# Attention and two feed-forward layers on one core: tails read back in halves, output weights copied two products later, outputs placed between products

## The chip, the cores and the metric

One core of one Trainium2 chip runs one program. The metric is the device time of an execution in microseconds, median of three runs. Products of full precision are built from split operands: every 32-bit operand is kept as a rounded half ("hi") and a remainder ("lo"), and a product takes three matmuls, hi·hi, hi·lo and lo·hi.

## The reference

```python
attn_out = _attn_ref(q, k, v, M_prev, z_prev, beta)        # 4 x 8 heads, 576 tokens, 64 wide
x = attn_out.transpose(0, 2, 1, 3).reshape(2304, 512)
h = x @ w_in;  x = np.maximum(0.01 * h, h) @ w_out         # first layers, 512 -> 2048 -> 512
a = x @ w_a;   b = x @ w_b
out = (a * b) @ w_out2                                     # second layers, 512 -> 1536 -> 512
```

## The kernel before

The program has three stages: attention (to about 200 us), the first layers (`moe1`, to about 583 us) and the second layers (`moe2`, to the end). TensorE runs the products, ScalarE (ACT) copies and rounds, VectorE (DVE) and GpSimd (POOL) add and subtract, and SyncE (SP) issues nearly all transfers. The order on each engine is the order in which the Python program emits the instructions; nothing reorders them. A counter, `tick()`, advances by one for each product or output on TensorE, and `after(k, ...)` emits a step k ticks later.

The 2304 tokens are worked in two parts, part one with 1024 tokens and part two with 1280.

**First layers.** `SETS` lists nine sets, each a part and one or two groups of 256 hidden columns. A set runs its inward products (kind "u", 12 matmuls each, chunk by chunk of 512 tokens) and then its outward products (kind "o"). The activations `x` of part two have a tail, the tokens from 1024 on, which lives in columns 0 to 1023 of a tile "g3". The same tile is the fourth hidden tile of the two-group sets, so the tail is kept in DRAM (`xkept`, 1 MB) and read back for each later set of part two: in `fourth(n)`, called when that set begins (L1476). The tail's first reader is the fifth inward product of such a set, the third chunk. The last set of part two keeps its tail in a tile inside `xs1` (`sums.first`).

**Second layers.** For each part, `slots(pr)` lists the order of work on TensorE. For q = 0 to 11 (even q: w_b, odd q: w_a of group g = q // 2) the letters 1 to 7 are seven products of 256 by 512 by 512 in Strassen's scheme with Winograd's sums, 6 matmuls each; "O" is one output of 128 tokens of the group before (also 6 matmuls, with the output weights), "T" a product of part two's last 256 tokens. After part one's q = 11 come the 8 outputs of group 5, O(5,0) to O(5,7), and then part two begins with two T.

- A product's result is summed on DVE (L1364) or, for product 1, copied from PSUM on ACT (L1368). When a block of an odd q is complete, DVE multiplies it with the block of w_b (L1391), and `finish` makes its halves: ACT rounds one tick later (L1348), DVE subtracts two ticks later (L1349). Product 7 completes block (f=1, c=1), 2 completes (0,0), 3 completes (1,0), 4 completes (0,1). An output of the first 512 tokens needs (0,0) and (1,0).
- The halves of a group lie in two of the three tiles hl0, hl1 and qs0, taken in rotation by `shared()`, so the second tile of a group is one that the outputs of the group before still read.
- `weights.final(g, ...)` brings the output weights of group g: two reads of 256 KB from DRAM into one small stage (L357), each followed by a copy on ACT (L358) and a subtraction on GpSimd (L359). It is called when the outputs of group g-2 are done.
- `Matrices.make` builds the split matrices of the later q on ACT (L1266) and GpSimd (L1263, L1270), writes them to DRAM (2 MB each, L1273, L1275), and part two reads them back (`fetch`, 2 MB each, L1291, L1292).
- The sums and halves of part two's inputs are jobs ("1b", "6", "5", "7c234"), put on a list at products of q = 11 and taken one a slot; their halves use ACT (L1174, L1175) and GpSimd (L1180, L1184).
- `xs1` holds the tail of part two in columns 0 to 2047 (`sums.tail`, made at the first product of q = 4, L1144 and L1148), and three inputs of products in the columns behind. The tail's first reader is part two's first T.

Of the kernel before, what the change touches and what calls it, by code (L numbers as in the profile page):

```python
# [11 lines left out]
F32 = mybir.dt.float32  # L12
F32R = mybir.dt.float32r
# [99 lines left out]
def f32(ap):  # L113
    return ap.bitcast(F32)
# [3 lines left out]
def attention_moe_moe2(ctx: ExitStack, tc, kqT, qn, vn, m_prev, beta, w_in, w_out, w_a, w_b, w_o2, out):  # L118
# [28 lines left out]
    def after(k, fn):  # L147
        now[1] += 1
        heapq.heappush(tasks, (now[0] + k, now[1], fn))
# [7 lines left out]
    class Weights:  # L157
# [194 lines left out]
        def final(self, g, t, stage):  # L352
            w = t.rearrange("p (s f c) -> p s f c", s=2, f=2)
            for f in range(2):
                k = max(0, self.staged - now[0])
                self.staged = now[0] + k + 8
                after(k, lambda f=f: nc.sync.dma_start(f32(stage), self.saved[g][:, f]))  # L357
                after(k + 5, lambda f=f: nc.scalar.copy(w[:, 0, f], f32(stage)))  # L358
                after(k + 6, lambda f=f: nc.gpsimd.tensor_tensor(w[:, 1, f], f32(stage), f32(w)[:, 0, f], ALU.subtract))  # L359
            return w  # L360

    SETS = [(0, [0]), (1, [0, 1]), (0, [1, 2]), (1, [2, 3]), (0, [3, 4]), (1, [4, 5]), (0, [5, 6]), (0, [7]), (1, [6, 7])]
# [693 lines left out]
    def shared(tag=None):  # L1056
        if tag is None:
            tag = gtags[count["g"] % len(gtags)]
            count["g"] += 1
        t = main.tile([P, 2 * WIDE], F32R, tag=tag, bufs=1, name=tag) if isinstance(tag, str) else tag()  # L1060
        return t.rearrange("p (s c) -> p s c", s=2)
# [57 lines left out]
    class Sums:  # L1119
# [8 lines left out]
        def first(self):  # L1128
            t = self.t1 = main.tile([P, 8192], F32R, tag="xh0", bufs=1, name="xs1")
            self.place(t, self.FIRST)  # L1130
            self.tail = t[:, 0:2048].rearrange("p (s k c) -> p s k c", s=2, k=4)
            self.g4 = t[:, 2048 : 2048 + 2 * WIDE].rearrange("p (s c) -> p s c", s=2)

        def second(self):
# [164 lines left out]
    def slots(pr):  # L1299

        tiles = (PARTS[pr + 1] - PARTS[pr]) // 128
        out = []
        for q in range(12):
            g, a = divmod(q, 2)
            if pr:
                text = ("16572O3O4OOOOTT", "1O6O5OO7234TT")[a] if g else ("TT1657234", "1657234TT")[a]
            else:
                text = ("16572O3O4OO", "1O6O5OO7234")[a] if g else "1657234"
            o, f = a * (tiles - 4), 0
            for x in text:  # L1310
                if x == "O":
                    out.append(("O", g - 1, o))
                    o += 1
                elif x == "T":
                    out.append(("T", q, f))
                    f += 1
                else:
                    out.append(("P", q, x))
        return out + [("O", 5, i) for i in range(tiles)]

    def moe2(ps, sums, mats, spare):
# [7 lines left out]
        for pr in range(2):  # L1329
# [10 lines left out]
            def into(g, f):  # L1340
                t = cts.setdefault(g, [None, None])
                if t[f] is None:
                    t[f] = shared()
                return t[f]

            def finish(g, f, c, gf):
# [100 lines left out]
    with tc.manual_schedule():  # L1447
        jobs = []

        def run(n):  # L1450
            for _ in range(min(n, len(jobs))):
                jobs.pop(0)()

        xh[0] = part_tile(main, "xh", 0, (2, 4), F32R)
        ps = ctx.enter_context(tc.tile_pool(name="ps", bufs=1, space=PSUM))
        with tc.tile_pool(name="att", bufs=1) as att:
            gates = attention(att, Plan(ps))
        sb = ctx.enter_context(tc.tile_pool(name="moe", bufs=1))
        weights.pool, weights.own, weights.n, weights.top = sb, 4, 4, 4
        weights.done |= {("own", i, h) for i in range(2) for h in range(2)}  # L1460
        x0, x1 = xh[0], sb.tile([P, 8192], F32R, tag="xh1", bufs=1, name="xh").rearrange("p (s k c) -> p s k c", s=2, k=4)
        xkept = dram.tile([P, 2, 1024], F32, tag="xkept", name="xkept")
        sums = Sums()
        credit = [0.0]
        t3s, ys = [None], {}

        def fourth(n):
            if n == len(SETS) - 1:
                sums.first()
                t = sums.g4  # L1470
            else:
                t = shared(lambda: sb.tile([P, 2 * WIDE], F32R, tag="g3", bufs=1, name="g3"))
            if SETS[n][0]:
                t3s[0] = t
                if n > 1:
                    nc.sync.dma_start(f32(t)[:, :, 0:1024], xkept)  # L1476
            return t

        def convert(w, rate):
            credit[0] += w * 1.33e-3 * rate * 2  # L1480
            while credit[0] >= 1:
                credit[0] -= 1
                weights.step()

        def x_of(s, kt, c):
            return t3s[0][:, s, kt * 256 : kt * 256 + 256] if c.start >= 1024 else x1[:, s, kt, c]

        def piece(kt, c, eng):
            nc.scalar.copy(x_of(0, kt, c), xf[1][:, kt, c])
            after(1, lambda: eng.tensor_tensor(x_of(1, kt, c), xf[1][:, kt, c], f32(x_of(0, kt, c)), ALU.subtract))  # L1490

        def y(pr):
            if pr not in ys:
                ys[pr] = part_tile(main, "xf", pr)
            return ys[pr]

        t31 = fourth(1)
        jobs += [lambda kt=kt, c=c: piece(kt, c, (nc.vector, nc.gpsimd)[kt % 2]) for c in chunks(1) for kt in range(4)]
        weights.spare += [("plain", m, h) for m in range(12) for h in range(2)] + [("last", g, h) for g in range(6) for h in range(2)]
        m = 0  # L1500
        xs = [lambda s, kt, c: x0[:, s, kt, c], x_of]
        for n, kind, g, w in moe1(ps, gates, lambda n: t31 if n == 1 else fourth(n), xs, y):
            if n == 1 and m == 0:
                m = 1
                nc.sync.dma_start(xkept, f32(t31)[:, :, 0:1024])
            if n == len(SETS) - 1:
                if (kind, g) == ("u", 6) and m == 1:
                    m = 2
                    raw = sb.tile([P, 2 * WIDE], F32, tag="g3", bufs=1, name="raw")
                    mats = Matrices(raw[:, 0:2048])  # L1510
                    mats.load(0)
                    mats.when = now[0]
                if kind == "o":
                    m += 1
                if m == 9:
                    mats.make(1)
                if m == 3:
                    while weights.items or weights.quarter or weights.spare:
                        weights.step()
                        tick()  # L1520
                    spares = [main.tile([P, 512], F32, tag=f"gf{i}", bufs=1, name="gf") for i in range(3)]
                    t = main.tile([P, 2 * WC], F32, tag="wraw", bufs=1, name="gf")
                    spares += [t[:, 0:WC], t[:, WC : 2 * WC]]
                    spares += [main.tile([P, WC], F32, tag=k, bufs=1, name="gf") for k in ("wh", "wa", "wr")]
                    sums.second()
                    mats.make(0)
                    steps = sums.jobs(ys[0], {f"S{i + 1}": spares[i * 2 : i * 2 + 2] for i in range(4)}, nc.vector)
                    jobs += [steps[k] for k in "a1b65c2d7"]
            run(2 if n == 0 else 1)
            convert(w, 0.7 if n == 0 else 0.74)  # L1530
        spares.append(raw[:, 2048:2560])
        y1 = ys[1]
        run(len(jobs))
        jobs += [steps[k] for k in "34"]
        for pr, (kind, q, k) in moe2(ps, sums, mats, spares):
            if (pr, kind, q, k) == (0, "P", 4, "1"):
                sums.last(y1)
                r = mats.raw
                steps = sums.jobs(y1, {
                    "S1": [y1[:, k, 512:1024] for k in range(2)],  # L1540
                    "S2": [r[:, k * 512 : k * 512 + 512] for k in range(2)],
                    "S3": [y1[:, k * 2 : k * 2 + 2, 1024:1280] for k in range(2)],
                    "S4": [r[:, k * 512 : k * 512 + 512] for k in range(2, 4)],
                }, nc.gpsimd)
            if (pr, kind, q, k) == (0, "P", 6, "1"):
                jobs += [steps["d"], steps["a"]]
            if (pr, kind, q) == (0, "P", 11):
                jobs += [steps[x] for x in {"1": "1b", "6": "6", "5": "5", "4": "7c234"}.get(k, "")]
            run(1)
        while tasks:  # L1550
            tick()
# [74 lines left out]
```

## Time and profile before

| | us |
|---|---|
| median of 3 runs | 1008.35 (1007.85 to 1008.89) |
| profiled execution, whole | 1009.16 |
| its span, first to last instruction | 1007.4 |
| TensorE busy in the span | 990.8 (98%) |
| granted TensorE clock, mean | 0.997 |

Matmuls of 512 columns overlap in the pipeline: each lasts 0.39 us in the trace and the next one starts 0.227 us after it. A place where TensorE loses time is therefore read from the distance between two starts. In a row of the timeline, a bracket tells how long the engine was idle before the instruction and what ended that.

### The profile page before, as it was taken

What the parts mean: (1) busy time and instruction counts of PE and PEld (TensorE: products, weight loads), DVE (VectorE), ACT (ScalarE), POOL (GpSimd) and SP (SyncE); (2) the same over time, 40 slices, a digit from 0 to 9 for tenths busy, and PEclk for the clock granted to TensorE, in tenths of its full rate; (3) what the DMA queues carried; (4) which work ended last, traced back from release to release, by engine and by line L of the source; (5) the groups of instructions that cost most, each with busy time, mean ns of one, the idle gap of its engine ahead of it and who ended that gap; (6) DMA issues with size and microseconds to landing.
All of it is one profiled execution on the core that took longest, in us unless ns stands there. A gap on an engine that the chain in (4) does not pass through costs nothing.

```text
span 1007.4 us, 14598 instructions
## 1 busy us (share of the span) xinstructions
PE 990.8 (98%) x5266; PEld 799.0 (79%) x5266; DVE 771.1 (77%) x1500; ACT 425.1 (42%) x947; POOL 378.6 (38%) x386
## 2 busy tenths in 40 slices
PE   9999999999999999999999999999998999999998
PEld 4666666788888888888888887887886888888887
DVE  6999999799797989798998764786665717647646
ACT  7988887465434333433335344323323122201201
POOL 6778777341111111111112787767577001001000
PEclk9999999999999999999999999999998999999999
DMA  7344432233535343435245337436554422432412
GB/s 233 103 134 139 139 124 67 71 108 109 154 111 169 114 136 106 172 111 156 88 154 178 115 136 256 176 132 230 219 197 180 178 94 95 167 115 94 144 45 105
DMA packets 41432, 139.88 MB, mean 139 GB/s; under 512 B 4752, under 2 KB 5520, under 8 KB 36752
## 3 DMA queue, kind: packets, MB, share of 16 engines
q1 hardware_dynamic: 41216, 138.95, 40.6%
q8 instruction: 41, 0.67, 0.3%
q14 instruction: 31, 0.25, 0.1%
q10 hardware_dynamic: 144, 0.00, 0.0%
HBM read 98.57 MB, written 40.37 MB: 138 GB/s over the span
## 4 chain that ended last, share of the span: by engine, by line
PE 86%; DVE 5%; DMA 3%; POOL 2%; ACT 2%; issue 1%; SPq 0%; ACTq 0%; POOLq 0%; DVEq 0%
PE b L373 24%; PE b L375 24%; PE b L374 24%; PE b L724 4%; PE b L803 3%; PE b L665 3%; PE b L775 1%; DVE gf L1364 1%; DMA g<-xkept 1%; PE b L596 1%; DMA qraw<-in_qn 1%; PE b L693 1%; DMA bhi<-saved 1%; DVE gf L1391 1%; ACT p L619 1%
## 5 line engine op out<-in xcount | busy, mean ns | idle before, releaser
L1364 DVE TENSOR_TENSOR gf<-b,gf 128x512 f32<-128x512 f32 x148 | 101.1, 688 | 77.1 <-PE b L375 66.2
L1426 DVE TENSOR_TENSOR xf<-b,xf 128x512 f32<-128x512 f32 (+1 forms) x91 | 62.2, 684 | 71.5 <-PE b L375 71.5
L1044 POOL TENSOR_TENSOR hl<-gf,hl 128x512 fp32r<-128x512 f32 (+1 forms) x20 | 28.3, 1415 | 234.9 <-ACT hl L1043 229.6
L359 POOL TENSOR_TENSOR w<-bhi,w 128x512 fp32r<-128x512 f32 x24 | 34.8, 1449 | 177.0 <-ACT w L358 167.6
L373 PE MATMUL b<-xh,w 128*128 128x512 f32 x256 | 100.9, 394 | 0.0
L374 PE MATMUL b<-xh,w 128*128 128x512 f32 x256 | 99.7, 390 | 0.0
L375 PE MATMUL b<-xh,w 128*128 128x512 f32 x256 | 99.7, 389 | 0.0
L373 PE MATMUL b<-xs,bhi 128*128 128x512 f32 (+1 forms) x216 | 79.4, 367 | 2.1 <-ACT gf L1368 1.7
L1077 ACT ACTIVATE gf<-b 128x512 f32<-128x512 f32 (+1 forms) x76 | 42.0, 553 | 89.5 <-PE b L375 88.5
L374 PE MATMUL b<-xs,bhi 128*128 128x512 f32 (+1 forms) x216 | 79.1, 366 | 0.0
L374 PE MATMUL b<-xs,ahi 128*128 128x512 f32 (+1 forms) x216 | 79.0, 366 | 0.0
L373 PE MATMUL b<-xs,ahi 128*128 128x512 f32 (+1 forms) x216 | 79.0, 366 | 0.0
L375 PE MATMUL b<-xs,blo 128*128 128x512 f32 (+1 forms) x216 | 79.0, 366 | 0.0
L375 PE MATMUL b<-xs,alo 128*128 128x512 f32 (+1 forms) x216 | 78.9, 365 | 0.0
L619 ACT ACTIVATE p<-p,stat 128x512 f32<-128x512 f32 (+3 forms) x128 | 71.0, 559 | 5.5 <-DVE stat L673 5.2
L646 POOL TENSOR_SCALAR p<-p,stat,keep 128x128 f32<-128x128 f32 (+3 forms) x95 | 61.0, 655 | 17.4 <-DVE stat L634 12.8
L261 ACT ACTIVATE wh<-wraw 128x512 f32<-128x512 f32 x64 | 42.7, 667 | 55.3 <-DMA wraw<-in_w_o 21.7
L373 PE MATMUL b<-hl,w 128*128 128x512 f32 (+1 forms) x176 | 65.2, 370 | 0.0
L374 PE MATMUL b<-hl,w 128*128 128x512 f32 (+1 forms) x176 | 65.1, 370 | 0.0
L375 PE MATMUL b<-hl,w 128*128 128x512 f32 (+1 forms) x176 | 65.1, 370 | 0.0
L673 DVE CUSTOM_DVE_ANT_0 p<-b,mask 128x512 f32<-128x512 f32 (+3 forms) x128 | 57.6, 479 | 5.4 <-PE b L665 5.0
L375 PE MATMUL b<-w,hl 128*128 128x512 f32 (+1 forms) x145 | 57.0, 393 | 2.0 <-DVE hl L1349 2.0
(204 smaller groups left out, 2669.0 us busy)
## 6 DMA issues: line engine op xcount, KB each, us to landing
wraw<-in_w_in SPq DMA_DIRECT2D x16, 512.0 KB, 4.0
wraw<-in_w_out SPq DMA_DIRECT2D x16, 512.0 KB, 3.4
qraw<-in_qn SPq DMA_DIRECT2D x8, 768.0 KB, 6.9
wraw<-in_w_b SPq DMA_DIRECT2D x12, 512.0 KB, 3.5
wraw<-in_w_a SPq DMA_DIRECT2D x12, 512.0 KB, 3.7
plain<-wa SPq DMA_DIRECT2D x24, 256.0 KB, 3.7
wraw<-in_w_o SPq DMA_DIRECT2D x12, 512.0 KB, 3.6
raw<-plain SPq DMA_DIRECT2D x12, 512.0 KB, 3.5
```

The source lines that it names most:

```text
L261: nc.scalar.activation(t["h"], self.raw[n][:, :, 1].bitcast(F32), AF.Abs)
L359: after(k + 6, lambda f=f: nc.gpsimd.tensor_tensor(w[:, 1, f], f32(stage), f32(w)[:, 0, f], ALU.subtract))
L373: nc.tensor.matmul(outp, l_hi, r_hi, start=start, stop=False)
L374: nc.tensor.matmul(outp, l_hi, r_lo, start=False, stop=False)
L375: nc.tensor.matmul(outp, l_lo, r_hi, start=False, stop=stop)
L619: nc.scalar.activation(t, t, AF.Exp, bias=s[:, 0, col : col + 1], scale=-1.0, accum_out=s[:, 1, col : col + 1])
L646: ENG[eng].tensor_scalar(live[p], live[p], stats[w % 3][:, 3, col : col + 1], k, ALU.mult, ALU.mult)
L673: nc.vector.tensor_tensor_reduce(one(p, [P, wd]), plan.tiles[banks[j]][:, c : c + wd], mask[:, off : off + wd], -0.125, BIG, ALU.add, ALU. ...
L724: nc.tensor.transpose(tt[0:kw, n * 128 : n * 128 + 128], live[name][:, kt * 128 : kt * 128 + kw], ident)
L1077: nc.scalar.activation(gf, hp[:, 0:n], AF.Prelu, alpha=0.01)
L1364: nc.vector.tensor_tensor(left[q, to], src, left[q, add], ALU.add)
L1426: nc.vector.tensor_tensor(y[:, i, c], op, y[:, i, c], ALU.add)
```

## The change

- `final`: the copy on ACT of a read of output weights is emitted 7 ticks after the read instead of 5, the subtraction after 8 instead of 6, and the reads are spaced by 10 ticks instead of 8.
- First layers: tile "g3" is one tile for the whole stage. Its tail is read back in two halves of 512 KB, one after the fourth and one after the eighth output of sets 2 and 4. For the last set, `sums.first()` and the read of the tail move to the first output of set 7.
- Second layers, part one, group 4: the first of its two tiles is no longer one of the rotation but columns 0 to 2047 of `xs1`. The tail of part two that lies there is written to DRAM (`tkept`, 1 MB) at the first product of q = 5 and read back after output O(4,7).
- q = 11 of part one: the order 1O6O5OO7234 becomes 1657O2O3O4O. The jobs "6" and "5" go on the list at product 4 and no longer at products 6 and 5.

```diff
@@ class Weights, final @@
-                self.staged = now[0] + k + 8
+                self.staged = now[0] + k + 10
                 after(k, lambda f=f: nc.sync.dma_start(f32(stage), self.saved[g][:, f]))
-                after(k + 5, lambda f=f: nc.scalar.copy(w[:, 0, f], f32(stage)))
-                after(k + 6, lambda f=f: nc.gpsimd.tensor_tensor(w[:, 1, f], f32(stage), f32(w)[:, 0, f], ALU.subtract))
+                after(k + 7, lambda f=f: nc.scalar.copy(w[:, 0, f], f32(stage)))
+                after(k + 8, lambda f=f: nc.gpsimd.tensor_tensor(w[:, 1, f], f32(stage), f32(w)[:, 0, f], ALU.subtract))
@@ class Sums, first @@
+            self.tkept = dram.tile([P, 2048], F32, tag="tkept", name="tkept")
@@ slots @@
-                text = ("16572O3O4OO", "1O6O5OO7234")[a] if g else "1657234"
+                text = ("16572O3O4OO", ("1O6O5OO7234" if g < 5 else "1657O2O3O4O"))[a] if g else "1657234"
@@ moe2, into @@
-                    t[f] = shared()
+                    here = pr == 0 and g == 4 and t == [None, None]
+                    t[f] = shared((lambda: sums.t1[:, 0:2048]) if here else None)
@@ main @@
+        longest = sb.tile([P, 2 * WIDE], F32R, tag="g3", bufs=1, name="g3").rearrange("p (s c) -> p s c", s=2)
         def fourth(n):
-            if n == len(SETS) - 1:
-                sums.first()
-                t = sums.g4
-            else:
-                t = shared(lambda: sb.tile([P, 2 * WIDE], F32R, tag="g3", bufs=1, name="g3"))
+            t = sums.g4 if n == len(SETS) - 1 else longest
             if SETS[n][0]:
                 t3s[0] = t
-                if n > 1:
-                    nc.sync.dma_start(f32(t)[:, :, 0:1024], xkept)
             return t
+        def tail_of_x(t, c0, c1):
+            nc.sync.dma_start(f32(t)[:, :, c0:c1], xkept[:, :, c0:c1])
...
         for n, kind, g, w in moe1(ps, gates, fourth, xs, y):
+            outs = outs + 1 if kind == "o" else 0
+            if n in (2, 4) and outs in (4, 8):
+                tail_of_x(longest, outs * 128 - 512, outs * 128)
+            if n == 7 and outs == 1:
+                sums.first()
+                tail_of_x(sums.g4, 0, 1024)
...
+            if (pr, kind, q, k) == (0, "P", 5, "1"):
+                nc.sync.dma_start(sums.tkept, f32(sums.t1)[:, 0:2048])
+            if (pr, kind, q, k) == (0, "O", 4, 7):
+                nc.sync.dma_start(f32(sums.t1)[:, 0:2048], sums.tkept)
...
             if (pr, kind, q) == (0, "P", 11):
-                jobs += [steps[x] for x in {"1": "1b", "6": "6", "5": "5", "4": "7c234"}.get(k, "")]
+                jobs += [steps[x] for x in {"1": "1b", "4": "657c234"}.get(k, "")]
```

## Rows read from the trace of the kernel before

**Rows 1.** The page, busy time, share of the span and instructions of each engine:

```profile
PE 990.8 (98%) x5266; PEld 799.0 (79%) x5266; DVE 771.1 (77%) x1500; ACT 425.1 (42%) x947; POOL 378.6 (38%) x386
```

**Rows 2.** Waits of TensorE, two longest: engine, line, waited for: us, times, longest

```profile
PE b L375 <- DVE hl L1349: 2.0, 1, 2.0
PE b L373 <- ACT gf L1368: 1.7, 1, 1.7
```

**Rows 3.** Timeline, set 3's tail: start, us, engine, line, operation, count, idle before

```profile
308.86 0.57 SPq L1476 DMA_DIRECT2D g<-xkept  x1
316.39 0.39 PE L375 MATMUL b<-xh,w 128*128 128x512 f32 x1
...
318.09 0.36 PE L373 MATMUL b<-g,w 128*128 128x256 f32 x1 [1.31 <-DMA g<-xkept]
```

**Rows 4.** Timeline, the tail of set 5:

```profile
409.08 0.52 SPq L1476 DMA_DIRECT2D g<-xkept  x1
...
416.54 0.39 PE L375 MATMUL b<-xh,w 128*128 128x512 f32 x1
418.40 0.35 PE L373 MATMUL b<-g,w 128*128 128x256 f32 x1 [1.48 <-ACT hl L1043]
```

**Rows 5.** Transfers: count, KB each, median us from issue to landing

```profile
bhi<-saved SPq DMA_DIRECT2D x24, 256.0 KB, 6.7
alo<-both SPq DMA_DIRECT2D x6, 1024.0 KB, 6.7
g<-xkept SPq DMA_DIRECT2D x2, 1024.0 KB, 9.1
```

**Rows 6.** Timeline around the start of q = 8, part one:

```profile
691.99 0.92 SPq L357 DMA_DIRECT2D bhi<-saved  x1
...
696.77 0.69 DVE L1391 TENSOR_TENSOR raw<-gf,raw 128x512 f32<-128x512 f32 x1
698.72 0.62 ACT L358 CAST w<-bhi 128x512 fp32r<-128x512 f32 x1 [1.49 <-DMA bhi<-saved]
699.77 0.58 ACT L1368 COPY gf<-b 128x512 f32<-128x512 f32 x1
700.40 0.50 PE L373 MATMUL b<-xs,bhi 128*128 128x512 f32 x1 [1.71 <-ACT gf L1368]
```

**Rows 7.** Timeline of TensorE, last products of q = 11 and first outputs of group 5:

```profile
751.08 0.39 PE L374 MATMUL b<-xs,ahi 128*128 128x512 f32 x1
754.71 0.39 PE L375 MATMUL b<-xs,alo 128*128 128x512 f32 x1
755.92 0.50 PE L373 MATMUL b<-w,qs 128*128 128x512 f32 x1 [0.82 <-ACT qs L1348]
760.73 0.80 PE L375 MATMUL b<-w,hl 128*128 128x512 f32 x1 [2.04 <-DVE hl L1349]
766.33 0.39 PE L373 MATMUL b<-w,qs 128*128 128x512 f32 x1
```

**Rows 8.** Stretches of 2 us: busy us (instructions) PE, PEld, DVE, ACT, POOL; clock; DMA share; GB/s

```profile
756.00:758.00 2.00, 0.93 (x3) 0.49 (x4) 1.97 (x4) 0.90 (x2) 0.00 (x0) 1.00 1.00 376
762.00:764.00 2.00, 2.00 (x6) 1.52 (x6) 1.59 (x2) 0.62 (x1) 2.00 (x2) 0.50 0.35 131
```

**Rows 9.** Page's costliest groups (busy, mean ns, idle before) for DVE's sums of products:

```profile
L1364 DVE TENSOR_TENSOR gf<-b,gf 128x512 f32<-128x512 f32 x148 | 101.1, 688 | 77.1 <-PE b L375 66.2
```

**Rows 10.** Timeline, DVE's subtractions without and with GpSimd at work:

```profile
756.99 0.69 DVE L1349 TENSOR_TENSOR qs<-gf,qs 128x512 fp32r<-128x512 f32 x1
758.32 3.48 POOL L1184 TENSOR_TENSOR xs<-xf,xs 128x512 fp32r<-128x512 f32 x2 [5.05 <-ACT xs L1175]
758.91 1.76 DVE L1349 TENSOR_TENSOR hl<-gf,hl 128x512 fp32r<-128x512 f32 x1
```

**Rows 11.** Timeline around the first output, O(0,0):

```profile
609.16 1.29 POOL L1270 TENSOR_TENSOR alo<-raw,ahi 128x512 fp32r<-128x512 f32 x1 [3.62 <-ACT ahi L1266]
...
611.00 0.39 PE L374 MATMUL b<-w,hl 128*128 128x512 f32 x1
```

More of the change, by code (lines that the diff above doesn't have):

```diff
@@ L1495, in y @@
             return ys[pr]
-        t31 = fourth(1)
+        t3s[0] = longest
         jobs += [lambda kt=kt, c=c: piece(kt, c, (nc.vector, nc.gpsimd)[kt % 2]) for c in chunks(1) for kt in range(4)]
         weights.spare += [("plain", m, h) for m in range(12) for h in range(2)] + [("last", g, h) for g in range(6) for h in range(2)]
-        m = 0
+        m, outs = 0, 0
         xs = [lambda s, kt, c: x0[:, s, kt, c], x_of]
-        for n, kind, g, w in moe1(ps, gates, lambda n: t31 if n == 1 else fourth(n), xs, y):
+        for n, kind, g, w in moe1(ps, gates, fourth, xs, y):
+            outs = outs + 1 if kind == "o" else 0
[4 more added lines that the diff above has]
+                tail_of_x(sums.g4, 0, 1024)
             if n == 1 and m == 0:
                 m = 1
-                nc.sync.dma_start(xkept, f32(t31)[:, :, 0:1024])
+                nc.sync.dma_start(xkept, f32(longest)[:, :, 0:1024])
             if n == len(SETS) - 1:
```

## The prediction

> **What bounds the kernel.** I read the page first: TensorE is busy 98% of the span [rows 1], so only a few us can be won, and only where TensorE waits. The waits of TensorE name the waiters in total [rows 2]; the timeline then gives each place, and there I count the distance between starts, which includes what follows a wait. The pitch is 16 matmuls in 3.63 us, 751.08 to 754.71 [rows 7], that is 0.227 us each, 1.36 us for a product or an output of six. After the attention stage four places lose more than 1 us:
>
> - Set 3's tail: 318.09 - 316.39 - 0.227 = 1.47 us, ended by the read of `xkept` [rows 3].
> - Set 5's tail: 418.40 - 416.54 - 0.227 = 1.63 us [rows 4]. The releaser named is an ACT copy, but the read was issued at 409.08, and with the 9.1 us that such a read takes [rows 5] it lands at 418.2, just ahead of the matmul. I take it for the same wait.
> - Start of q = 8: about 1.7 us [rows 6].
> - From the last product of q = 11 into the outputs of group 5: from 754.71 to 766.33 lie 19 steps, 11.62 us where 19 x 0.227 = 4.31 would do: 7.31 us lost [rows 7]. After 760.73 there are 13 steps in 5.60 us instead of 2.95, so 2.65 us of the loss is the clock: the granted clock is 0.50, the 1.2 GHz level, behind the three waits [rows 8]. The other three places show no such fall after one wait of 1.3 to 1.7 us.
>
> Together 12.1 us.
>
> **The change, part by part.**
>
> *Tail in halves: +3.1 us.* In order on SP the first half is issued behind the fourth output of sets 2 and 4, four outputs (4 x 12 x 0.227 = 10.9 us) before the set's end, and the second right behind the eighth. Even issued at 308.86 and as slow as the whole (9.1 us [rows 5]), the second half would land no later than the whole does now. But its issue now stands ahead of the load of weights that held SP until then, so it goes out when the last output ends, about 306.3 by the pitch (fifth inward product's start, 316.62, less four inward products of 2.72, plus 0.6 for the last matmul and the semaphore). At 9.1 us it lands at 315.4, at half the size (4.6 us) at 310.9; TensorE asks at 316.62. Both waits go: 1.47 + 1.63. Bounds: 1.5 (if ACT was the cause at 418) and 3.1. SP now stands waiting for an output with the weight loads queued behind it; those are paced by DVE, which waits for the same output first. Cost: nothing, since the weights run a set ahead; without that cover one transfer of 512 KB, some 4.6 us by the row above. The read for the last set only moves earlier past some loads; no wait stands there today, so nothing.
>
> *Output weights two ticks later: +1.3 us at q = 8, -0.2 us elsewhere.* At q = 8 the read went out at 691.99 behind 2 MB of matrices, took 6.7 us [rows 5, 6], and the copy L358 kept ACT until it landed. Behind it on ACT stood one rounding copy, then L1368, which frees the PSUM tile that TensorE waits for. With the copy elsewhere, ACT's next two start when DVE is done, 696.77 + 0.69 = 697.46: L1368 at about 698.1 (L358 to L1368 is 1.05 for two copies [rows 6], so 0.53 for one), TensorE 0.63 later at 698.7, against 700.40 - 1.71 = 698.69 due. The wait of 1.7 goes. Against it: by the new spacing another read's subtraction (tick 78, counted from the start of the second layers) falls among DVE's last steps of q = 7. What GpSimd does to a DVE subtraction is seen at 756.99 and 758.91: 0.69 alone, 1.76 beside GpSimd's work [rows 10]. I take 0.4 off, between 0 and 1.07: 1.3.
>
> The GPSIMD Engine Reference of the Trainium skill (Specifications) says that GpSimd shares its memory interface with VectorE and contends with instructions of two inputs there. By that rule every moved GpSimd step could cost a DVE step 1.07, and the trace agrees for the pair above.
>
> The other reads: the later copy stands nearer to its use. The nearest is the second half of the first output weights, subtraction at tick 18, O(0,0) at tick 20. On GpSimd it now queues behind L1270 at 609.16, ends at 609.16 + 2 x 1.29 = 611.7, and TensorE wants it at 611.00 [rows 11]: 0.7 us late. Its old place beside DVE's subtractions comes free, which can give up to 1.07 back. I take -0.2, bounds -0.8 and +1.1. All later weights have 4 ticks or more (5.4 us) in hand.
>
> *Outputs between products, tile in `xs1`, jobs later: +6.5 us.* Let 0 be the start of O(5,0). Today O(5,0) directly follows products 3 and 4, whose halves it needs; DVE is then 5 to 6 us behind. In the new order product 3 ends 3 slots and product 7 seven slots earlier, at -9.52. From there DVE has, up to the last half O(5,0) needs: 3 steps for product 7, 2 each for 2 and 3, three outputs' additions and three subtractions, 13 x 0.69 = 9.0 us [rows 9, 10], starting some 0.3 behind TensorE: end at -0.2. O(5,0) needs that half with its sixth matmul, at 1.1. So DVE just holds. GpSimd still has the job "1b" and one half of output weights beside the first of these steps; two slowed by 1.07 make 2.1, less the 1.3 in hand: 0.8 us. The halves of product 4 are wanted by O(5,4) 5.4 us later and have that slack. One wait of 0.8 is less than the three places that leave the clock up, so the 2.65 us come back too: 7.3 - 0.8 = 6.5, bounds 0 and 7.3.
>
> Jobs "6", "5" and the rest now run from product 4 on: on GpSimd seven pieces of 2.6 to 3.5 us (two instructions each [rows 10]) end at 17 to 23; part two's products that need them start at 15 (S2, ready first) to 22 (the last). Hidden at the lower price, 1 us at the upper, inside the range.
>
> The write of `tkept` (1 MB) at q = 5 adds some 2.8 us to the transfers at the rate of 376 GB/s [rows 8]; behind it on SP stand a read of output weights and a read of a raw matrix with more than 5 us in hand. The read back stands behind the 2 MB fetch for q = 13 and ahead of output weights and the stores of results. It may start at 0; the first T needs it 8 outputs later, at 10.9. At 376 GB/s, 3.15 MB from about -1.4 end at 7: hidden, with 3.9 us in hand. Nothing else on SP waits there that TensorE needs.
>
> **Sum.** 3.1 + 1.3 - 0.2 + 6.5 = 10.7 us. Against the span: 1007.4 to 996.7; against the profiled execution 1009.16 to 998.5; that execution stood 0.8 above the median, so the median goes from 1008.35 to 997.6. The best of all bounds, 3.1 + 1.7 + 1.1 + 7.3 = 13.2, gives 995.2.
>
> **The rivals.**
>
> *DVE becomes the bound at the seam.* If all six of its subtractions and multiplications there are slowed by 1.07, O(5,0) waits 6.4 - 1.3 = 5.1 us, and the clock falls again, 2.65: the seam gains nothing and 4.2 remain, 1004.1; with three slowed and the clock falling, 7.3 - 1.9 - 2.65 = 2.75 at the seam and 1001.4. For: rows 10. Against: GpSimd has been emptied there by the later jobs.
>
> TensorE: Matmul & The Clock Gate of the Trainium skill (HAM oscillation) warns that waiting matmuls drop to half rate and pay for it after the wait; the trace agrees for the seam, at 0.50 [rows 8], and not for single waits of 1.3 to 1.7 us.
>
> *The read back is late, moderately.* If only the 1 MB runs as slowly as `xkept` did (9.1 us, rows 5) behind the fetch at 4.2, it lands at 13.3 and T waits 2.4 us: 1000.0.
>
> *Slower than before.* If the whole 3.15 MB run at the rate of `xkept`, 1.05 MB in 9.1 us, they land at 26, T waits 15 us and the clock falls: 17.7 lost against 10.7 won, 1015.3. It decides from a landing at about 19, less than 154 GB/s. Against: the same fetch runs at 376 GB/s [rows 8] and such 1 MB pieces land in 6.7 us [rows 5].
>
> *The halves don't end both waits.* If the second tail was held by the ACT copy [rows 4], 1.6 less is won: 999.2.
>
> **How the numbers follow.** Forecast 0.70 (995.2 to 999), the ACT copy 0.05, late read back 0.09, DVE at the seam 0.12, slower 0.04. I predict 997.6. The range 995.0 to 1002.0 takes in the bounds, the moderate read back and half of the DVE case. About 2 us (0.2%) is what a measurement can tell. Faster by more than that: all but the slower case and 0.01 of the DVE case, 0.95; within it 0.02; slower 0.03.
>
> **What would show it.** In the new trace: no wait of TensorE for `xkept`; at the start of q = 8 no idle time before product 2; between product 4 of q = 11 and the T of part two 9 outputs at a pitch of 0.227 with the granted clock at 1.00; the read of `tkept` landing less than 10.9 us after O(4,7). It would be wrong with a T waiting for the read back, with a granted clock of 0.5 anywhere at the seam, or with O(0,0) waiting more than 1 us for its weights.

## The result, and the profile after

The changed kernel takes 996.88 us (median of 4 runs, 996.54 to 997.46), the kernel before 1008.57 beside it: 11.7 us less, ratio 0.9886 with a 95% interval of 0.9869 to 0.9903. A second set of runs gave 997.14 and 0.9889. The span of the profiled execution went from 1007.4 to 995.3 us.

The page of the changed kernel, busy time of the engines and granted clock in 40 slices; TensorE's share was 98% [rows 1], and its busy time is 3.8 us shorter with the same 5266 instructions. The matmuls at the lower clock account for 2.65 us of that; the rest goes with the waits, as a matmul that no other overlaps is busy for its whole 0.39 us:

```profile
PE 987.0 (99%) x5266; PEld 797.8 (80%) x5266; DVE 770.9 (77%) x1500; ACT 425.1 (43%) x947; POOL 377.2 (38%) x386
PEclk9999999999999999999999999999999999999999
```

The waits of TensorE, three longest. The two of [rows 2] are gone; the only new one, third in the list, is for output weights (L359). The first two lie in the attention stage:

```profile
PE b L397 <- POOL mask L381: 1.6, 1, 1.6
PE b L596 <- DVE stat L630: 0.6, 1, 0.6
PE b L374 <- POOL w L359: 0.6, 1, 0.6
```

Timeline of the changed kernel at the tail of set 3, to be read beside [rows 3]. The second half goes out at 305.69 where the whole went out at 308.86, and the first matmul on the tail starts 0.23 us after the one before it, the ordinary pitch:

```profile
305.69 0.52 SPq L1478 DMA_DIRECT2D g<-xkept  x1
...
316.15 0.39 PE L375 MATMUL b<-xh,w 128*128 128x512 f32 x1
316.38 0.28 PE L373 MATMUL b<-g,w 128*128 128x256 f32 x1
```

Timeline at the start of q = 8, beside [rows 6]. No copy L358 stands ahead of L1370 (L1368 before), and TensorE starts 0.38 us after its last matmul (0.15 more than the pitch) where it was 2.10:

```profile
688.69 0.32 SPq L357 DMA_DIRECT2D bhi<-saved  x1
...
693.71 0.69 DVE L1393 TENSOR_TENSOR raw<-gf,raw 128x512 f32<-128x512 f32 x1
694.96 0.58 ACT L1370 COPY gf<-b 128x512 f32<-128x512 f32 x1
695.59 0.50 PE L373 MATMUL b<-xs,bhi 128*128 128x512 f32 x1
```

Timeline at the seam before part two, beside [rows 7]. O(5,0) starts at 750.12, with no idle time. DVE's subtraction of product 3's block ends at 750.42 + 0.69 = 751.11, and the sixth matmul, which needs it, starts at 751.25. From 750.12 to the first T at 761.05 lie 48 steps in 10.93 us, 0.228 each:

```profile
750.12 0.39 PE L373 MATMUL b<-w,hl 128*128 128x512 f32 x1
750.31 0.32 SPq L1555 DMA_DIRECT2D xs<-tkept  x1
750.42 0.69 DVE L1351 TENSOR_TENSOR hl<-gf,hl 128x512 fp32r<-128x512 f32 x1
751.25 0.42 PE L375 MATMUL b<-w,hl 128*128 128x512 f32 x1
...
761.05 0.28 PE L373 MATMUL b<-xs,bhi 128*128 128x256 f32 x1
```

DVE's steps for that block start at 740.80 without a break, and two of them are slowed beside GpSimd (part of the timeline):

```profile
740.80 1.42 DVE L1366 TENSOR_TENSOR gf<-b,gf 128x512 f32<-128x512 f32 x2 [0.67 <-PE b L375]
742.25 1.74 DVE L1393 TENSOR_TENSOR raw<-gf,raw 128x512 f32<-128x512 f32 x1
743.39 1.75 POOL L359 TENSOR_TENSOR w<-bhi,w 128x512 fp32r<-128x512 f32 x1
744.68 1.02 DVE L1351 TENSOR_TENSOR hl<-raw,hl 128x512 fp32r<-128x512 f32 x1
```

The transfers of the changed kernel (count, KB each, median us to landing). The read back of `tkept` lands at 750.31 + 7.6 = 757.9, 3.1 us before the first T:

```profile
g<-xkept SPq DMA_DIRECT2D x4, 512.0 KB, 4.4
xs<-tkept SPq DMA_DIRECT2D x1, 1024.0 KB, 7.6
```

Stretches of 2 us at the seam, columns as in [rows 8], where the second row showed a clock of 0.50. The seam now lies between 750 and 761, and the clock is 1.00 in each stretch of it; the first row here has the start of O(5,0):

```profile
750.00:752.00 2.00, 2.00 (x11) 1.54 (x10) 1.88 (x4) 1.43 (x3) 1.01 (x1) 1.00 0.94 257
756.00:758.00 2.00, 2.00 (x10) 1.65 (x10) 1.63 (x3) 0.53 (x1) 2.00 (x2) 1.00 0.98 386
```

Timeline at O(0,0), beside [rows 11]. GpSimd's half of the weights, queued behind L1271 (L1270 before), ends at 606.46 + 1.28 = 607.74, and TensorE waits for it:

```profile
606.46 1.28 POOL L359 TENSOR_TENSOR w<-bhi,w 128x512 fp32r<-128x512 f32 x1
607.80 0.50 PE L374 MATMUL b<-w,hl 128*128 128x512 f32 x1 [0.57 <-POOL w L359]
```

### The profile page after: what moved, and what is told of

Its sections match the earlier page's. It is cut to its first block, busy times and chain, and to the rows that moved or that the text cites. A ratio compares the mean times of both kernels' runs of the same rounds, so it can differ in the third digit from the quotient of the medians.

```text
span 995.3 us, 14603 instructions
## 1 busy us (share of the span) xinstructions
PE 987.0 (99%) x5266; PEld 797.8 (80%) x5266; DVE 770.9 (77%) x1500; ACT 425.1 (43%) x947; POOL 377.2 (38%) x386
## 4 chain that ended last, share of the span: by engine, by line
PE 91%; DVE 3%; POOL 2%; ACT 1%; issue 1%; DMA 1%; POOLq 0%; DVEq 0%
PE b L373 26%; PE b L374 26%; PE b L375 26%; PE b L724 4%; PE b L803 3%; PE b L665 3%; PE b L775 1%; PE b L596 1%; ACT p L619 1%; PE b L693 1%; POOL alo L1271 1%; POOL raw L1264 1%; DVE p L673 1%; POOL p L646 0%; DMA raw<-in_kqT 0%
## 5 line engine op out<-in xcount | busy, mean ns | idle before, releaser
L359 POOL TENSOR_TENSOR w<-bhi,w 128x512 fp32r<-128x512 f32 x24 | 32.9, 1369 | 170.5 <-ACT w L358 163.4
```

Source lines behind the costliest of these rows:

```text
L359: after(k + 8, lambda f=f: nc.gpsimd.tensor_tensor(w[:, 1, f], f32(stage), f32(w)[:, 0, f], ALU.subtract))
```

## The experiments

### Each part of the change alone

The theory: the three parts win at different places and nearly add up.

**The tails.** The edits of `fourth`, `longest` and `tail_of_x`, in the kernel before; nothing else.

> The kernel before with the tail's edits alone. Theory (both tail waits were the read of xkept): 1.47 + 1.63 = 3.1 us less than before, about 1005.4, and no idle time of TensorE at the third chunk of sets 3 and 5. Rival (the second wait was the ACT copy that the trace names): 1.5 us less, about 1007.1, and the wait at set 5 stays.

Measured: 1004.64 us against 1007.77, 3.1 us less, ratio 0.9967 (0.9956 to 0.9978). Both tail waits are gone from the trace, the one for which an ACT copy was named too. The losses at q = 8 and at the seam stand, the seam's at 6.3 us instead of 7.3, because the clock stays at its lower level for a shorter time in this execution. That the last set's read moved too is in all three kernels with the tail's edits and not tested by itself; no trace, before or after, has a wait there.

**The output weights.** Only the distances in `final`:

```diff
-                self.staged = now[0] + k + 8
+                self.staged = now[0] + k + 10
-                after(k + 5, ...copy...)
-                after(k + 6, ...subtract...)
+                after(k + 7, ...copy...)
+                after(k + 8, ...subtract...)
```

> The kernel before with the output weights' new distances alone. Theory: the 1.7 us at the start of q = 8 go but for some 0.3, and O(0,0) waits 0.6 to 0.9 us for GpSimd's half of its weights: 0.5 to 1.1 us less than before, about 1007.7; the seam before part two is as it was, with the clock at half. Rival (the new wait at O(0,0) costs as much as the old one gave): no change.

Measured: 1006.85 against 1007.77, 0.9 us less, ratio 0.9991 (0.9982 to 0.9999), just clear of no change. The trace is plainer than the time: in it the distance between starts at q = 8 fell from 2.10 to 0.40, and O(0,0) has the new wait, 0.99 instead of 0.23.

**The seam.** Own tile, `tkept`, the order of q = 11 and the late jobs, with the old distances of the weights and the old tails.

> The kernel before with the second layers' edits alone (own tile, tkept, order of q = 11, jobs later). Theory: the whole loss at the seam goes, 7.3 us less than before, about 1001.2, granted clock 1.00 throughout. Rival (the seam only gains once the other waits are gone, or part is given back at the first T): 4 to 6 us less.

Measured: 1001.01 against 1007.77, 6.8 us less, ratio 0.9932 (0.9919 to 0.9944), the granted clock at 1.00 throughout. Nothing is left of the loss at the seam. Elsewhere the trace shows one new loss. Its timeline at the start of q = 6: the write of `tkept` stands ahead of a read of output weights on SP, the copy L358 now waits 1.01 us for it, and TensorE loses 0.46 us behind it. In the kernel before that copy did not wait.

```profile
666.76 0.62 ACT L358 CAST w<-bhi 128x512 fp32r<-128x512 f32 x1 [1.01 <-DMA bhi<-saved]
668.44 0.50 PE L373 MATMUL b<-xs,bhi 128*128 128x512 f32 x1 [0.30 <-ACT gf L1370]
```

In the whole change this wait is missing. There the read behind the write goes out at 650.58 and takes 7.5 us, so it lands 0.8 us ahead of its copy, which is less than the two ticks (2.7 us) that the copies come later:

```profile
650.58 1.03 SPq L357 DMA_DIRECT2D bhi<-saved  x1
658.90 0.62 ACT L358 CAST w<-bhi 128x512 fp32r<-128x512 f32 x1
```

So the later copies also pay for `tkept`. The three parts sum to 3.1 + 0.9 + 6.8 = 10.8 of the 11.7 us; the rest lies within the intervals. The new wait doesn't explain it: in the same trace the distance at q = 8 is 1.47 where it was 2.10, which gives about as much back.

### What in the tail's edits counts

Two things changed at once: the read is halved, and it is issued ahead of a load of weights. Two kernels take them apart. The first reads the whole 1 MB at the new place:

```diff
-            if n in (2, 4) and outs in (4, 8):
-                tail_of_x(longest, outs * 128 - 512, outs * 128)
+            if n in (2, 4) and outs == 8:
+                tail_of_x(longest, 0, 1024)
```

> As e1_tails, but the tail is read back whole (1 MB), in one read right behind the eighth output. Theory A (it is enough that the read no longer stands behind a load of weights on SP): issued at about 305.7, it lands within 9.1 us at 314.8, ahead of 316.6: 3.1 us less than before, as e1_tails. Theory B (the halving is what counts): the wait stays in good part, 0 to 1.5 us less than before.

The second reads halves, the second of them at the old place, in `fourth(n)`:

```diff
+                if n in (3, 5):
+                    tail_of_x(t, 512, 1024)
...
-            if n in (2, 4) and outs in (4, 8):
-                tail_of_x(longest, outs * 128 - 512, outs * 128)
+            if n in (2, 4) and outs == 4:
+                tail_of_x(longest, 0, 512)
```

> The kernel before with the tail's edits, but the second half of the tail issued where the whole read stood before, at the start of the set and so behind a load of weights on SP. It tells whether the halving alone is enough, as the place alone was. Theory C (either is enough): the second half, 512 KB and 4.4 us as measured in the changed kernel, goes out at about 308.5 and lands at 313, ahead of 316.6: 3.1 to 3.3 us less than before. Rival (the halving does nothing by itself): no change.

Measured: whole at the new place 1004.23 against 1007.77, ratio 0.9966 (0.9954 to 0.9979); halves with the second at the old place 1004.86 against 1008.13, ratio 0.9972 (0.9960 to 0.9983). Neither trace has a tail wait left, so each edit alone is enough. The transfers show why; first the whole read, then the halves:

```profile
305.22 0.57 SPq L1476 DMA_DIRECT2D g<-xkept  x1
g<-xkept SPq DMA_DIRECT2D x2, 1024.0 KB, 5.6
```

```profile
308.49 0.52 SPq L1478 DMA_DIRECT2D g<-xkept  x1
g<-xkept SPq DMA_DIRECT2D x4, 512.0 KB, 5.2
```

At the new place the whole read takes 5.6 us and not 9.1 [rows 5]; the 512 KB of weights that were issued 0.4 us ahead of it now stand behind it. Whether the queue or the traffic beside the read cost the 3.5 us, these runs don't separate. The second half at the old place takes 6.0 us (the median above takes in the early first halves) and lands at 314.5; the whole at the new place lands at 311.1. The whole at the old place landed at 317.9, and TensorE asks at about 316, so either edit gains more than the wait was, and the place leaves more in hand.

### Which part of the second layers' edits wins at the seam

**Old order.** The changed kernel with q = 11 as before; own tile and late jobs stay:

```diff
-                text = ("16572O3O4OO", ("1O6O5OO7234" if g < 5 else "1657O2O3O4O"))[a] if g else "1657234"
+                text = ("16572O3O4OO", "1O6O5OO7234")[a] if g else "1657234"
```

> The changed kernel with the order 1O6O5OO7234 of q = 11 put back; own tile, tkept and the late jobs stay. Theory (the order is what wins at the seam): O(5,0) waits again, 3.4 us (GpSimd out of the way) to 4.4, and with the half clock up to 7.3: 1000.3 to 1004.2 us. Rival (the tile of its own or the later jobs win it): below 998.

Measured: 1002.76 against 1007.1, ratio 0.9956 (0.9939 to 0.9972), 5.6 to 5.9 us slower than the changed kernel by the medians, 6.7 to 7.1 by the ratios. The timeline and the stretches of 2 us have the old picture: O(5,0) waits for DVE's subtractions, the last time for 2.05 us, and the clock falls to 0.50. Summed over the distances between starts, 6.7 us are lost there.

```profile
754.63 0.79 PE L375 MATMUL b<-w,hl 128*128 128x512 f32 x1 [2.05 <-DVE hl L1351]
```

```profile
756.00:758.00 2.00, 2.00 (x6) 1.54 (x5) 1.51 (x2) 1.10 (x2) 2.00 (x2) 0.50 0.36 135
```

So the order wins; without it the own tile and the late jobs together recover some 0.6 of the 7.3 us. That the own tile is what allows the order follows from the rotation of the tiles (the new order writes the second half of group 5 while outputs of group 4 are still to come); no run has the order without the tile.

**Early jobs.** The changed kernel with the jobs put back:

```diff
-                jobs += [steps[x] for x in {"1": "1b", "4": "657c234"}.get(k, "")]
+                jobs += [steps[x] for x in {"1": "1b", "6": "6", "5": "5", "4": "7c234"}.get(k, "")]
```

> The changed kernel with jobs 6 and 5 put back to products 6 and 5 of q = 11. Theory (GpSimd's halves slow DVE's steps between the last products, where only 0.1 us is in hand): O(5,0) waits 1.5 to 4 us, 998.4 to 1001 us; if that brings the clock down, 2.65 more. Rival (GpSimd's work beside DVE doesn't matter there): 996.9 as the changed kernel.

Measured: 999.57 against 1007.1, ratio 0.9928 (0.9913 to 0.9943), 2.4 to 2.7 us above the changed kernel by the medians, 3.9 to 4.2 by the ratios. The trace shows the wait within O(5,0), 2.17 us between starts:

```profile
744.79 1.14 ACT L1176 CAST xs<-xf 128x512 fp32r<-128x512 f32 x2
745.83 0.62 ACT L1350 CAST hl<-raw 128x512 fp32r<-128x512 f32 x1
746.49 0.73 DVE L1351 TENSOR_TENSOR hl<-raw,hl 128x512 fp32r<-128x512 f32 x1 [1.62 <-ACT hl L1350]
...
753.01 0.50 PE L373 MATMUL b<-w,hl 128*128 128x512 f32 x1 [1.78 <-ACT hl L1350]
```

The size is as expected, the cause only in part. Three of the four executions kept a mean clock of 1.000, the slowest (1001.4) has 0.998. DVE first loses 1.62 us to ACT: the rounding copies of the jobs (L1176), with a copy of weights among them, stand in ACT's queue ahead of product 7's (L1350). In the changed kernel the same L1350 starts at 744.02, 1.8 us earlier in the span, some 1.5 in TensorE's own time. GpSimd beside DVE adds the rest: three of DVE's later steps take 1.01 to 1.07 us instead of 0.69.

### How much the read back of the tail has in hand

Idle writes of 1 MB each to DRAM are issued on SP just ahead of the read back, two in one kernel and five in another; their data are not used.

```diff
+                for i in range(2):
+                    nc.sync.dma_start(dummy[i], y1[:, :, 0:512])
                 nc.sync.dma_start(f32(sums.t1)[:, 0:2048], sums.tkept)
```

> The changed kernel with two idle writes of 1 MB each to DRAM on SP's queue just ahead of the read back of tkept. Theory (transfers of that place run at about 400 GB/s): the read lands 5.3 us later, at 763.2, the first T waits 2.2 us: 999.1 us, clock at 1.00. Rival (large slack, other order of landing): no change. Rival (slow queue, as xkept's 115 GB/s): 10 us or more later.

> As e7_late2 with five idle writes of 1 MB. Theory: the read lands 13.1 us later, at 771.0, the first T waits 10 us, and the clock then stands at its lower level for a while, 2.65 us more as at the seam of before: 1009.5 us, no faster than the kernel before. Rival (the clock does not fall for one wait): 1006.9 us.

Measured with two: 1001.41 (999.68 to 1002.79) against 1007.1, ratio 0.9942 (0.9928 to 0.9957). In the profiled execution, the fastest, the first T starts 2.40 us after the matmul before it, 2.17 more than the pitch, and the clock stays at 1.00:

```profile
763.66 0.36 PE L373 MATMUL b<-xs,bhi 128*128 128x256 f32 x1 [2.00 <-DMA xs<-tkept]
```

So the wait was as expected, 2.2 us, but the median is 2.3 us above the 999.1 expected. The other three executions took 1.3 to 3.1 us longer, and their mean granted clock is 0.998 where it is 1.000 in the first. It is likely that the clock fell behind this wait in them; there is no trace of them, so neither the place nor the length of their wait is shown.

Measured with five: 1009.37 (1008.29 to 1013.3), ratio 1.0028 (1.0015 to 1.0041), slower than the kernel before. The first T waits 9.88 us, and the clock falls during the wait and is back some 3.5 us after its end (stretches of 2 us, columns as in [rows 8]):

```profile
764.00:766.00 2.00, 0.00 (x0) 0.00 (x0) 0.00 (x0) 0.00 (x0) 2.00 (x3) 0.66 1.05 407
772.00:774.00 2.00, 2.00 (x12) 2.00 (x11) 0.00 (x0) 0.62 (x1) 1.14 (x1) 0.50 1.05 404
774.00:776.00 2.00, 2.00 (x15) 2.00 (x15) 0.00 (x0) 0.37 (x1) 0.14 (x1) 0.78 1.06 409
```

So the end of the slower rival, a late read back with a lower clock behind it, can be brought about: with 2 MB more in the queue the change still wins 5.7 us, with 5 MB it wins nothing. Its premise, transfers at the slow rate of `xkept`, does not show: the stretches above run at 404 to 409 GB/s.

### A version that beats both

The second read of the first output weights follows after 8 ticks again:

```diff
-                self.staged = now[0] + k + 10
+                self.staged = now[0] + k + (10 if self.staged else 8)
```

> The changed kernel, but the second read of the first output weights follows the first after 8 ticks and no longer 10, so that its GpSimd half stands ahead of L1271's first piece of the next matrix. Theory: the wait of O(0,0) for L359 (0.73 us by the starts, and 0.1 after it) goes: 996.1 us. Rival (the half now stands beside DVE's subtractions at the end of q = 1 and delays product 2 instead): 996.9, no change, with the loss at another matmul.

> The changed kernel itself again on the same chip, for the comparison with e9_first8: 996.9 us. Theory: e9_first8 lies 0.8 us below it. Rival: both alike.

Measured on one chip: 995.77 (995.39 to 996.18), ratio 0.9876 (0.9858 to 0.9894), beside 997.14 (996.58 to 997.32), ratio 0.9889 (0.9873 to 0.9904). The four runs of the one all lie below the four of the other. The half of the weights is done at 602.57 + 1.83 = 604.4, before O(0,0) starts:

```profile
602.57 1.83 POOL L359 TENSOR_TENSOR w<-bhi,w 128x512 fp32r<-128x512 f32 x1 [5.06 <-ACT w L358]
```

The gain is 1.4 us where 0.8 was expected. The rest of the loss at q = 8 went too. In the changed kernel, run beside it, a multiplication of DVE starts 0.19 us behind GpSimd's L359 and takes 1.65 us (first pair); here it starts 0.64 us behind and takes 1.20 (second pair):

```profile
687.54 1.29 POOL L359 TENSOR_TENSOR w<-bhi,w 128x512 fp32r<-128x512 f32 x1 [0.27 <-ACT w L358]
687.73 1.65 DVE L1393 TENSOR_TENSOR gf<-gf 128x512 f32<-128x512 f32 x1
```

```profile
685.84 1.29 POOL L359 TENSOR_TENSOR w<-bhi,w 128x512 fp32r<-128x512 f32 x1 [0.29 <-ACT w L358]
686.48 1.20 DVE L1393 TENSOR_TENSOR gf<-gf 128x512 f32<-128x512 f32 x1
```

As the spacing counts on, later reads of part one are emitted two ticks (2.7 us) earlier, but these 0.45 us are all that is left of it here, and which step on SP or in the transfer sets them was not followed.

## Why the prediction was right

It gave 997.6 and 10.7 us won; 996.88 and 11.7 were measured. By its steps:

- **What bounds.** The four places held 12.1 us; all four are gone or nearly so, and TensorE's list of waits after 200 us has one entry. It was not quite all that could be won: the version with 8 ticks stands 12.4 us below the kernel before, as it also ends some losses of less than 1 us around O(0,0).
- **The tails, +3.1.** Right in size, and the second wait was the read's, as taken, though the trace named ACT. What the working did not say is that either of the two edits does it; its bound for the new place, 9.1 us, would have covered the whole read, which takes 5.6 there.
- **The output weights, +1.3 at q = 8.** The two starts stood 2.10 apart and are now 0.38 apart: 1.7 won. The 0.4 taken off for GpSimd beside DVE is there (1.65 us for a step of 0.69), but only 0.15 us of it reached TensorE.
- **The first weights, -0.2.** 0.7 us late was worked out from the queue of GpSimd, 0.73 came. The relief of DVE that was set against it came only in small part: of the two starts of 0.49 and 0.54 us just before, one of 0.47 is left. The net is -0.4.
- **The seam, +6.5.** Too low by 0.8. The steps of DVE were counted right: the 13 run from 740.80 to 751.11, and without what GpSimd added they take 8.9 us where 9.0 were worked out. The term that was mis-sized is GpSimd beside DVE: two steps were slowed, as forecast, to 1.74 and 1.02 us, which adds 1.4 us and not 2.1. So the 0.8 us of wait didn't come, and 0.14 us were left at the sixth matmul of O(5,0). That is close: the early jobs show what a little more costs. The clock's 2.65 us came back in full.
- **`tkept`.** Write and read back were priced at nothing. For the read back that held: 3.1 us in hand where 3.9 were worked out. For the write it held only because of the later copies: the read of output weights behind it was given more than 5 us in hand and had 0.8. With the old copies the write costs a wait of 0.46 us (the seam alone).

Of the rivals, DVE as the bound at the seam is what the early jobs show, through ACT first; the late read back and the slower case are what two and five idle writes show, with the waits that were expected of them (2.2 and 10 us). With the terms as measured, 3.1 + 1.7 - 0.4 + 7.3 gives the 11.7 us: three of the four errors are under 0.5 us, and no two large ones cancel.

## What to carry to other kernels

Where the busiest engine works 98% of the time, list the distances between its starts: the loss sat in four places, and the price of each could be read to 0.2 us, the time at the lower clock included. A consumer that directly follows the last producer pays for the whole chain behind it; putting independent work between the last steps wins that back, but the rounding and subtracting of other data must leave the same engines' queues at that point, and a buffer must be found that allows the new order. A read that lands late can be cured by its place in the queue as well as by its size; here the place left more in hand.

## What the runs showed of the hardware

The granted clock fell from 1.00 to 0.50 during waits of TensorE or right behind them, but not at one length of wait. By the idle times in the brackets, single waits of 1.3 to 1.7 us left it at 1.00 (kernel before), and so did one of 1.8 (early jobs) and one of 2.0 (two idle writes) in the profiled executions. Of the eight executions of these two kernels, four have a mean clock of 1.000 and four of 0.998; as the waits of those without a trace are not known, it stays open whether the same wait goes either way or theirs were longer. One wait of 9.9 us brought the clock down before it was over. Three waits close together brought it down in the kernel before (0.8, 1.1 and 2.0 us within 6.0) and with the old order (0.1, 1.2 and 2.05 us within 5.4). TensorE: Matmul & The Clock Gate of the Trainium skill (Part 1, What's actually happening) describes two levels, full rate when busy and half rate after idling. The rows show these two levels; they also show that a single wait of 2.0 us can leave the clock up where one as long, with two shorter ones just ahead of it, does not.

At one place, what GpSimd costs DVE went by how far the two overlapped: a step of DVE on 128x512 takes 0.69 us alone [rows 10]; the one at q = 8 took 1.65 us when it started 0.19 us behind a GpSimd step of 1.29 us, and 1.20 us when it started 0.64 us behind.
